# Weight preparation spread over later stages in a one-core attention and MLP kernel

## The chip, the cores and the metric

The kernel runs on one core of a Trainium2 chip. The metric is the device time of one execution in microseconds (us); lower is better. A core has a matrix engine (TensorE, PE in the profile, its weight loads PEld), a vector engine (VectorE, DVE), a scalar engine (ScalarE, ACT), GpSimd (POOL) and SyncE (SP), which here issues almost all transfers. Each engine works through its own queue of instructions in order and waits for the others by semaphores.

## The reference

Eight batches with twelve heads of 448 x 64: queries and keys are normed by their root mean square, attention runs on them, and the result (3584 rows of 768) goes through an MLP with `h - tanh(h)` between its two layers.

```python
q_n, k_n = (rmsnorm(q, g_q), rmsnorm(k, g_k))
scores = scale * np.matmul(q_n, k_n.transpose(0, 1, 3, 2))
attn = np.exp(scores - max); attn = attn / (np.sum(attn) + 1e-09)
attn_out = np.matmul(attn, v)
x = attn_out.transpose(0, 2, 1, 3).reshape(B * S, H * D)
...
h = x @ w_in            # 768 x 2048
g = h - np.tanh(h)
out = (g @ w_out)       # 2048 x 768
```

The two weights come as float64, read as pairs of 32-bit words.

## The kernel before, in words

**Attention in slots.** A slot is one pair of heads of one batch; there are 48 (`steps`). The first six (batch 0) run in `first_slot`, the next six (batch 1) in `early_slot`, the rest in `slot`. A slot holds scores, exponentials, totals (L700, their reciprocal `rs` on VectorE L705), the products with v, and for later slots the loads of q, k and v, the norm (`rr`, L143 to L145, with a power on GpSimd) and the transposes on TensorE (L467, L471). The recording order in the code is the order on each engine; nothing reorders it.

**The MLP as a stream.** `mlp()` is a generator that yields after each matmul. `run(gap)` inside a slot takes so many nanoseconds of it. For the eight batches the stream is hidden(0), project_first(0), hidden(1), project(1), and then pairs of batches. The layers, except project_first, are made from seven products per block (a Strassen-like scheme; `ORDER` is 1, 5, 6, 2, 3, 7, 4), so each needs sums and differences of weight blocks, the combinations. hidden(0) has four sets of seven products; each product is 6 matmuls, 12 instructions on TensorE, and it goes to one of three PSUM banks called mm. Slots 6, 7 and 8 carry hidden(0); slots 9, 10 and 11 carry project_first.

**Preparing the weights.** There are 32 pieces (`PIECES`): 0 to 15 of w_in, 16 to 31 of w_out. Each is loaded raw (768 KB, L290 or L294), passes ScalarE twice (L71, L72), VectorE three times (`round_weight_b`, L78, L79, L82) and GpSimd twice (L92). `weight(to)` starts pieces up to `to`: it puts ScalarE's part of piece n, then by `settle(n)` the VectorE and GpSimd parts of the piece before it, then the loads of pieces ahead. Raw data lies in the later gT buffer for the first `EARLY` pieces, after that in three rotating buffers `w_raw`; a buffer is free again when GpSimd is done with its piece. When four w_in pieces are settled, four combinations are queued (`combine`, L357). The finished w_in blocks are kept in DRAM (`keep_step`, L372), for all later batches.

`EARLY` is 8: `first_slot` asks for pieces up to s + 2, that is 7 by the end of slot 5. In hidden(0) the list `due` says up to which piece the weights are asked for at each of the 28 products: 8 at the first, 16 at the 14th, 24 at the last.

**project_first.** Six chunks of 128 output columns, each summed over 16 row blocks f: 96 matmuls (L1339, two instructions each). Before, chunk follows chunk, the right three first, each in one mm bank: right half from pieces 16 to 23, left half from 24 to 31. Pieces 24 to 31 are asked for over the first 48 matmuls; then `combine_w_out` (L381 to L384) makes four combinations of w_out rows for each of eight f, one f every four matmuls, in two slots of the ring, and they are kept in DRAM (L388). After each chunk ScalarE copies the bank, VectorE transposes it (L966) and SP stores it (four issues, L971).

**The ring.** `ring` has six slots (`SLOTS`). From hidden(1) on every product reads its weights from a ring tile that is loaded from DRAM some products ahead (`ring_load`, issued by SP). Before, project_first loads the first four tiles at matmuls 84 and 86, and each product of hidden(1) then asks for five tiles more than its own number.

**Totals.** In `visit`, used from slot 11 on, slots 11 and 12 take an mm bank for their totals.

Of the kernel before, what the change touches and what calls it, by code (L numbers as in the profile page):

```python
# [147 lines left out]
def bounded_path(tc, ctx, q, k, v, moe_w_in, moe_w_out, out, g_col, ident, ones, half_ones, neg_half, early):  # L148
# [17 lines left out]
    nc = tc.nc  # L166
    B, H, S, D = q.shape
# [47 lines left out]
    def mm_bank():  # L215
        return bank_of("mm")
# [170 lines left out]
    def keep_factors(n, count, f, src):  # L387
        nc.sync.dma_start(  # L388
            out=w_out_dram[:, n : n + count, :, f, :].rearrange("p k c d -> p (k c) d"),
            in_=src[:, : count * HALF].rearrange("p (k d) -> p k d", d=P),  # L390
        )
# [25 lines left out]
            ring_steps += [(first, 2, p, part) for p in outer for part in (1, 2, 3, 4, 0)]  # L417
    ring_tiles = {}

    def ring_load(to):  # L420

        for n in range(len(ring_tiles), min(to, len(ring_steps))):
            b, layer, j, p = ring_steps[n]
            t = ring_tiles[ring_steps[n]] = ring_slot()
            if layer == 0:
                assert kept[1] > j
                nc.sync.dma_start(out=t[:, : 2 * HALF], in_=w_in_dram[j, p])
            elif layer == 2 and p == 0:
                nc.sync.dma_start(out=t, in_=w_out_dram[:, BLOCKS[j], HC - 1].rearrange("p f d -> p (f d)"))
            elif layer == 2:  # L430
                n = min(2 * HB, 7 * HB - 2 * (p - 1) * HB)
                at = 2 * (p - 1) * HB
                nc.sync.dma_start(out=t[:, :n], in_=inner_dram[j][:, at : at + n])
            else:
                nc.sync.dma_start(out=t, in_=w_out_dram[:, BLOCKS[p], j].rearrange("p f d -> p (f d)"))


    normed, turned, probs, sums, whole, xT, tt = {}, {}, {}, {}, {}, {}, {}
# [208 lines left out]
    def visit(s, av):  # L647
# [169 lines left out]
    assert len(due) == 7 * SETS and due[-1] == CF + HF  # L817

    def part(name):
        if name == "th" and "blocks" in late:  # L820
# [60 lines left out]
    def hidden(b):  # L881
# [25 lines left out]
        def done_with(j):  # L907
# [11 lines left out]
            def use(p, bank):  # L919
# [2 lines left out]
                    beside_hidden(b, j, p)  # L922
                if p == 1:
                    nc.scalar.copy(out=s1, in_=v)
                elif p == 5:
                    nc.vector.tensor_tensor(out=s5, in0=v, in1=s1, op=ALU.add)
# [382 lines left out]
    def project_first(b):  # L1309
# [4 lines left out]
        late["todo"] = []  # L1314
        keep_step(0, SETS - 1)
        took = 4 * S / ENGINE_NS
        for m in range(CD * CF):
            k, f = m // CF, m % CF
            n = (k + HC) % CD
            if f == 0:  # L1320
                bank = mm_bank()
            if f == CF // 2:
                step_out(2)
            if k < HC:
                weight(CF + HF + HF * (m + 1) // (HC * CF))
            elif m < HC * CF + 2:
                keep_w_out(PIECES - 2 + m - HC * CF)
            elif (m - HC * CF) % 4 == 0 and m - HC * CF <= 4 * HF:
# [79 lines left out]
    def first_slot(s):  # L1408
# [471 lines left out]
```

## Time and profile before

| what | value |
|---|---|
| median of 3 runs | 1344.65 us (1343.43 to 1344.74) |
| profiled execution, time | 1342.53 us |
| its span on the core | 1340.7 us |
| PE busy | 1311.5 us, 98% |
| DVE busy | 969.5 us, 72% |
| ACT busy | 568.1 us, 42% |
| POOL busy | 795.0 us, 59% |
| TensorE clock granted, mean | 0.998 |
| first six slots on PE | until about 76 us |
| hidden(0) on PE | 76.7 to 172.9 us |
| project_first on PE | 176.3 to 268.6 us |
| hidden(1) starts on PE | 274.5 us |

A busy share is a mean over stages with different limits, so it tells little by itself. A row of a timeline reads: start, length, engine, line, operation, output<-input, shape, count, and in brackets how long the engine had been idle before and what ended that. A row of waits reads: engine, line, tile, what it waited for, then the sum in us, how often, and the longest. A row of windows gives for each engine the busy time and the number of instructions in the stretch, then the granted TensorE clock (1.00 is full speed), the share of the DMA engines that was busy, and GB/s.

### The profile page before, as it was taken

The numbers are of one execution on the slowest core, as the hardware profiler recorded it, in microseconds if no ns is written. First come the engines' busy times: TensorE is split into PE (matmuls) and PEld (weight loads), VectorE is DVE, ScalarE is ACT, GpSimd is POOL, SyncE is SP. The second block draws the span as 40 slices with busy tenths as digits, with TensorE's granted clock in tenths as the row PEclk, the third lists the DMA queues.
The fourth block names the chain that finished last, engine by engine and source line by source line (L and its number), as shares of the span: only waits on it lengthen the run. The fifth ranks groups of instructions, "written<-read, shape, count | busy, mean of one in ns | idle before, by whom it ended". The sixth has DMA issues, their size and how long they took to land.

```text
span 1340.7 us, 29301 instructions
## 1 busy us (share of the span) xinstructions
PE 1311.5 (98%) x11368; PEld 1033.4 (77%) x11368; DVE 969.5 (72%) x1410; ACT 568.1 (42%) x1328; POOL 795.0 (59%) x591
## 2 busy tenths in 40 slices
PE   7989999999999999999999999999999999999997
PEld 3467854488998888688878788779887888799986
DVE  4999978867765767688888576768888667634455
ACT  7856654244343454445322445454512254311102
POOL 4766776348846256726698245944699244812771
PEclk9999999999999999999999999999999999999999
DMA  7779889889999766476655867466745776466544
GB/s 169 183 214 262 265 260 231 250 278 279 340 284 287 181 160 180 112 186 155 171 149 136 201 162 183 117 170 165 181 132 145 150 201 161 118 161 172 170 142 102
DMA packets 364759, 253.53 MB, mean 189 GB/s; under 512 B 273028, under 2 KB 303300, under 8 KB 364612
## 3 DMA queue, kind: packets, MB, share of 16 engines
q1 hardware_dynamic: 364608, 251.57, 69.1%
q8 instruction: 92, 1.51, 0.5%
q14 instruction: 55, 0.45, 0.1%
q10 hardware_dynamic: 4, 0.00, 0.0%
HBM read 205.23 MB, written 46.27 MB: 188 GB/s over the span
## 4 chain that ended last, share of the span: by engine, by line
PE 83%; DVE 7%; POOL 4%; DMA 2%; SPq 2%; issue 2%; ACT 1%; DVEq 0%; ACTq 0%; POOLq 0%
PE mm L857 38%; PE mm L1142 21%; PE sc L569 9%; PE sc L635 6%; PE mm L1339 5%; POOL u L1099 3%; PE sc L623 1%; POOL rr_mine L523 1%; PE sc L677 1%; DVE w_out L357 1%; PE mm L677 1%; SPq L497 1%; DVE rs L705 1%; DMA w_f<-w_inner 1%; DVE w_out L82 0%
## 5 line engine op out<-in xcount | busy, mean ns | idle before, releaser
L857 PE MATMUL mm<-xT,w_f 128*128 128x224 f32 x1296 | 263.5, 353 | 0.8 <-DVE xT L767 0.8
L857 PEld LDWEIGHTS mm<-xT,w_f 128*128 128x128 f32 x1296 | 244.8, 190 | 5.5 <-issue 4.2
L569 PE MATMUL sc<-qT,kT 64*32 64x448 f32 (+1 forms) x3072 | 215.6, 499 | 2.7 <-ACT p_last L575 2.1
L857 PE MATMUL mm<-tt,w_f 128*128 128x224 f32 x1044 | 212.6, 355 | 0.2 <-DMA w_f<-w_in 0.2
L857 PEld LDWEIGHTS mm<-tt,w_f 128*128 128x128 f32 x1044 | 195.8, 190 | 15.9 <-issue 15.4
L523 POOL TENSOR_TENSOR rr_mine<-rr_mine,neg_half 128x28 f32<-128x28 f32 x33 | 162.2, 4915 | 2.7
L762 DVE TENSOR_TENSOR xT<-xT,sc 128x448 f32<-128x448 f32 x34 | 21.0, 618 | 165.8 <-PE sc L569 114.8
L1142 PE MATMUL mm<-u,w_f 128*128 128x224 f32 x672 | 137.2, 354 | 1.0 <-POOL u L1099 0.5
L905 POOL TENSOR_TENSOR gT<-s,th 128x448 f32<-128x448 f32 x44 | 57.8, 1313 | 132.2 <-ACT th L904 128.7
L1142 PE MATMUL mm<-gT,w_f 128*128 128x224 f32 (+3 forms) x512 | 132.0, 412 | 1.2 <-DVE acc L1149 0.9
L1142 PEld LDWEIGHTS mm<-u,w_f 128*128 128x128 f32 x672 | 126.1, 190 | 8.0 <-POOL u L1099 3.6
L569 PEld LDWEIGHTS sc<-qT,kT 64*32 64x32 f32 x3072 | 72.4, 106 | 68.1 <-issue 49.2
L1142 PEld LDWEIGHTS mm<-gT,w_f 128*128 128x128 f32 x512 | 93.9, 190 | 34.3 <-issue 32.0
L635 PE MATMUL sc<-p,v_nat 64*32 64x448 f32 x1184 | 116.9, 536 | 0.0
L1142 PE MATMUL mm<-g,w_f 128*128 128x224 f32 (+1 forms) x360 | 98.9, 428 | 0.0
L575 ACT ACTIVATE p<-sc 128x448 f32<-128x448 f32 x132 | 71.9, 545 | 50.3 <-PE sc L569 37.4
L905 POOL TENSOR_TENSOR g<-s,th 128x448 f32<-128x448 f32 x24 | 30.3, 1264 | 105.1 <-ACT th L904 105.1
L1142 PEld LDWEIGHTS mm<-g,w_f 128*128 128x128 f32 x360 | 67.9, 190 | 26.5 <-issue 26.0
L729 ACT COPY sum_g<-sum 32x14 f32<-32x14 f32 x280 | 56.3, 201 | 72.0 <-DVE sum L721 66.3
L1339 PE MATMUL mm<-gT,w_out 128*128 128x448 f32 x192 | 74.0, 542 | 0.0
L145 POOL TENSOR_TENSOR rr<-rr,neg_half 112x8 f32<-112x8 f32 (+1 forms) x30 | 49.8, 1689 | 35.5 <-DVE rr L144 35.0
L1099 POOL TENSOR_TENSOR u<-gT 128x448 f32<-128x448 f32 x48 | 63.5, 1342 | 11.1 <-PE mm L1142 11.1
(206 smaller groups left out, 2465.8 us busy)
## 6 DMA issues: line engine op xcount, KB each, us to landing
w_f<-w_in SPq DMA_DIRECT2D x196, 384.0 KB, 3.5
w_f<-w_inner SPq DMA_DIRECT2D x63, 512.0 KB, 3.7
w_f<-w_out SPq DMA_DIRECT2D x42, 512.0 KB, 3.9
w_raw<-in_moe_w_out_dram SPq DMA_DIRECT2D x16, 768.0 KB, 5.4
w_in<-w_out SPq DMA_DIRECT2D x21, 384.0 KB, 5.3
qk_nat<-in_q_dram SPq DMA_DIRECT2D x132, 56.0 KB, 2.6
qk_nat<-in_k_dram SPq DMA_DIRECT2D x132, 56.0 KB, 2.4
g<-w_out SPq DMA_DIRECT2D x14, 512.0 KB, 5.4
```

The costliest lines, as they stand in the source:

```text
L145: nc.gpsimd.tensor_tensor(out=r, in0=r, in1=neg_half[:rows], op=ALU.pow)
L523: nc.gpsimd.tensor_tensor(out=mine, in0=mine, in1=neg_half[:, :1].to_broadcast([P, 2 * NJ]), op=ALU.pow)
L569: nc.tensor.matmul(tiles[h][i * BL : (i + 1) * BL, :n], lhsT=kT[r, c * P + at : c * P + at + BL], rhs=qT[r, first : first + n], start=True ...
L575: nc.scalar.activation(p[:, h, c if c < 2 else 0, :], tiles[h][:, :n], AF.Exp, scale=1.0 if rr is None else rr[:, 0, 2 * c + h : 2 * c + h ...
L635: nc.tensor.matmul(av[g][i * BL : (i + 1) * BL, :S], lhsT=v_nat[keys, h, c, m * BL : (m + 1) * BL], rhs=p[keys, h], start=first, stop=True ...
L677: nc.tensor.matmul(av[n][r : r + BL, :HS], lhsT=v_nat[:, h, c, m * BL : (m + 1) * BL], rhs=p[c][:, h, n * HS : (n + 1) * HS], start=False, ...
L729: nc.scalar.copy(out=acc[h * BL : (h + 1) * BL, g], in_=part[g * BL : (g + 1) * BL, h * NJ : (h + 1) * NJ])
L857: nc.tensor.matmul(bank[:, f * HS : (f + 1) * HS], lhsT=w[:, c * width + f, :], rhs=moving[p](c), start=(first and f == 0 and c == 0), sto ...
L905: eng.tensor_tensor(out=g[:, rows, cols], in0=h, in1=th, op=ALU.subtract)
L1099: nc.gpsimd.tensor_tensor(out=u[:, half], in0=a[:, half], in1=z[:, half], op=ALU.subtract)
L1142: nc.tensor.matmul(bank[:, :n], lhsT=w(i), rhs=mv, start=(first and i == 0), stop=(i == len(moving) - 1), skip_group_check=not first,)
L1339: nc.tensor.matmul(bank[:, :S], lhsT=w_out_row(f, n // HC)[:, n % HC * P : (n % HC + 1) * P], rhs=g[:, f, :], start=(f == 0), stop=(f == C ...
```

## The change

- `EARLY` is 5. `first_slot` starts pieces 0 to 4 in slots -1 to 3 and none in slots 4 and 5; `settle` is called in the slot itself.
- `due` in hidden(0) is a list by a new rule: 5 5 6 7 8 8 8, 9 9 10 10 11 12 12, 13 13 14 14 15 16 16, 17 17 18 18 19 19 19. So 14 pieces beside the first layer.
- The last 13 pieces are asked for in project_first by the list `behind`, over its first 58 matmuls.
- project_first works on three chunks at once: for each row block f one matmul into each of the three mm banks, first for the right half, then for the left. The combinations of w_out rows start six matmuls later (58 to 86). The last two of them are written to DRAM in four pieces each instead of two. The three results of a half are copied and stored together.
- The totals of slots 11 and 12 take an sc bank.
- Ring tiles: two are loaded at matmul 92, six by matmul 94, and three more are issued by ScalarE in the first set of hidden(1).

```diff
-    EARLY, PIECES = 8, 2 * CF
+    EARLY, PIECES = 5, 2 * CF
...
-        late["keep"].append(lambda: [keep_factors(3 + 2 * i, 2, f, t[i]) for i in range(2)])
+        if f < HF - 2:
+            late["keep"].append(lambda: [keep_factors(3 + 2 * i, 2, f, t[i]) for i in range(2)])
+            return
+        late["keep"].append(lambda: [keep_factors(3 + n, 1, f, s) for n, s in enumerate((s3, s1, s2, s4))])
...
-    def ring_load(to):
+    def ring_load(to, queue=nc.sync):
...
-            totals(s, mm_bank())
+            totals(s, sc_bank())
...
-    due = [EARLY + (CF - EARLY) * (m + 1) // (7 * SETS // 2) for m in range(7 * SETS // 2)]
-    due += [CF + HF * (m + 1) // (7 * SETS // 2) for m in range(7 * SETS // 2)]
+    SOON_OUT, LAST_OUT = 3, 58
+    due = [min(EARLY + max(m - 1, 0), 8 + max(m - 5, 0) * 4 // 7, CF + SOON_OUT) for m in range(7 * SETS)]
+    behind = [min(PIECES, CF + SOON_OUT + (PIECES - CF - SOON_OUT) * (m + 1) // LAST_OUT) for m in range(CD * CF)]
...
                 if p == 1:
                     nc.scalar.copy(out=s1, in_=v)
+                    if single and j == 0:
+                        ring_load(SLOTS + 1, nc.scalar)
...
                     nc.vector.tensor_tensor(out=s2, in0=v, in1=s1, op=ALU.add)
+                    if single and j == 0:
+                        ring_load(SLOTS + 2, nc.scalar)
                 elif p == 2:
                     shrink(up, low, v, nc.vector)
+                    if single and j == 0:
+                        ring_load(SLOTS + 3, nc.scalar)
...
         for m in range(CD * CF):
-            k, f = m // CF, m % CF
-            n = (k + HC) % CD
-            if f == 0:
-                bank = mm_bank()
-            if f == CF // 2:
-                step_out(2)
-            if k < HC:
-                weight(CF + HF + HF * (m + 1) // (HC * CF))
...
-                combine_w_out((m - HC * CF) // 4 - 1)
-            elif m == CD * CF - 12:
-                ring_load(2)
...
-            elif m == CD * CF - 10:
-                ring_load(4)
+            k, f, i = m // (HC * CF), m % (HC * CF) // HC, m % HC
+            n = (1 - k) * HC + i
+            if m % 4 == 3:
+                step_out()
+            weight(behind[m])
+            if f == 0:
+                bank = [] if i == 0 else bank
+                bank.append(mm_bank())
...
+            if m >= LAST_OUT - 4:
+                keep_combined((m - LAST_OUT + 4) // 4)
...
+            if m == CD * CF - 4:
+                ring_load(2)
+            elif m == CD * CF - 2:
+                ring_load(SLOTS)
             nc.tensor.matmul(
-                bank[:, :S], lhsT=w_out_row(f, n // HC)[:, n % HC * P : (n % HC + 1) * P], rhs=g[:, f, :],
+                bank[i][:, :S], lhsT=w_out_row(f, n // HC)[:, n % HC * P : (n % HC + 1) * P], rhs=g[:, f, :],
                 start=(f == 0), stop=(f == CF - 1),
             )
             if f == CF - 1:
-                y = part("s2").rearrange("p f s -> p (f s)")
-                nc.scalar.copy(out=y, in_=bank[:, :S])
-                store(b, n, y)
+                y = part(("s2", "s5", "s1")[i]).rearrange("p f s -> p (f s)")
+                nc.scalar.copy(out=y, in_=bank[i][:, :S])
+                store(b, n, y, part("s2").rearrange("p f s -> p (f s)") if i == 2 else None)
...
-            weight(s + 2)
+            weight(min(s + 2, EARLY))
+            settle(min(max(s + 1, 0), EARLY))
```

More of the change, by code (lines that the diff above doesn't have):

```diff
@@ L426, in ring_load @@
                 assert kept[1] > j
-                nc.sync.dma_start(out=t[:, : 2 * HALF], in_=w_in_dram[j, p])
+                queue.dma_start(out=t[:, : 2 * HALF], in_=w_in_dram[j, p])
             elif layer == 2 and p == 0:
-                nc.sync.dma_start(out=t, in_=w_out_dram[:, BLOCKS[j], HC - 1].rearrange("p f d -> p (f d)"))
+                queue.dma_start(out=t, in_=w_out_dram[:, BLOCKS[j], HC - 1].rearrange("p f d -> p (f d)"))
             elif layer == 2:
@@ L432, in ring_load @@
                 at = 2 * (p - 1) * HB
-                nc.sync.dma_start(out=t[:, :n], in_=inner_dram[j][:, at : at + n])
+                queue.dma_start(out=t[:, :n], in_=inner_dram[j][:, at : at + n])
             else:
-                nc.sync.dma_start(out=t, in_=w_out_dram[:, BLOCKS[p], j].rearrange("p f d -> p (f d)"))
+                queue.dma_start(out=t, in_=w_out_dram[:, BLOCKS[p], j].rearrange("p f d -> p (f d)"))
     normed, turned, probs, sums, whole, xT, tt = {}, {}, {}, {}, {}, {}, {}
@@ L812, in bounded_path @@
     late = {}
[L815 to L817 removed]
+    SOON_OUT, LAST_OUT = 3, 58
+    due = [min(EARLY + max(m - 1, 0), 8 + max(m - 5, 0) * 4 // 7, CF + SOON_OUT) for m in range(7 * SETS)]
+    behind = [min(PIECES, CF + SOON_OUT + (PIECES - CF - SOON_OUT) * (m + 1) // LAST_OUT) for m in range(CD * CF)]
+    assert due[-1] == CF + SOON_OUT and due[7 * (SETS - 1) - 2] == CF
     def part(name):
@@ L1316, in project_first, with keep_combined @@
         took = 4 * S / ENGINE_NS
-        for m in range(CD * CF):
-            k, f = m // CF, m % CF
-            n = (k + HC) % CD
-            if f == 0:
-                bank = mm_bank()
-            if f == CF // 2:
-                step_out(2)
-            if k < HC:
-                weight(CF + HF + HF * (m + 1) // (HC * CF))
-            elif m < HC * CF + 2:
-                keep_w_out(PIECES - 2 + m - HC * CF)
-            elif (m - HC * CF) % 4 == 0 and m - HC * CF <= 4 * HF:
+        combined = [0]
+        def keep_combined(to):
+            for f in range(combined[0], min(to, HF)):
                 for fn in late["keep"]:
@@ L1331, in project_first @@
                 late["keep"] = []
-                combine_w_out((m - HC * CF) // 4 - 1)
-            elif m == CD * CF - 12:
-                ring_load(2)
+                combine_w_out(f)
+                combined[0] = f + 1
+        for m in range(CD * CF):
+            k, f, i = m // (HC * CF), m % (HC * CF) // HC, m % HC
[6 more added lines that the diff above has]
+                bank.append(mm_bank())
+            if LAST_OUT <= m < LAST_OUT + 2:
+                keep_w_out(PIECES - 2 + m - LAST_OUT)
+            if m >= LAST_OUT - 4:
+                keep_combined((m - LAST_OUT + 4) // 4)
+            if m == CD * CF - 6:
                 for fn in late["keep"]:
                     fn()
-            elif m == CD * CF - 10:
-                ring_load(4)
+                late["keep"] = []
+            if m == CD * CF - 4:
+                ring_load(2)
+            elif m == CD * CF - 2:
+                ring_load(SLOTS)
             nc.tensor.matmul(
-                bank[:, :S], lhsT=w_out_row(f, n // HC)[:, n % HC * P : (n % HC + 1) * P], rhs=g[:, f, :],
+                bank[i][:, :S], lhsT=w_out_row(f, n // HC)[:, n % HC * P : (n % HC + 1) * P], rhs=g[:, f, :],
                 start=(f == 0), stop=(f == CF - 1),
```

## The prediction

> **What bounds the kernel now.** I read the windows first, then who TensorE waited for, then the timelines of the engines around the places found. All times are microseconds of the profiled execution, counted from the start of its span.
>
> ```profile
> core 0: us, PE busy (x) PEld busy (x) DVE busy (x) ACT busy (x) POOL busy (x), PEclk, DMA share, GB/s
> 60.00:70.00 10.00, 8.48 (x164) 4.15 (x167) 9.71 (x15) 7.78 (x14) 9.24 (x8) 1.00 0.82 194
> 80.00:90.00 10.00, 7.04 (x40) 6.34 (x38) 9.76 (x12) 5.72 (x9) 4.66 (x5) 1.00 1.00 284
> 90.00:100.00 10.00, 8.85 (x111) 5.66 (x112) 9.86 (x13) 1.86 (x5) 6.32 (x5) 0.83 0.42 151
> 110.00:120.00 10.00, 8.38 (x88) 6.26 (x80) 9.83 (x13) 4.43 (x12) 9.11 (x7) 1.00 0.98 276
> 140.00:150.00 10.00, 10.00 (x100) 7.83 (x99) 9.79 (x15) 4.20 (x12) 8.06 (x6) 1.00 0.92 290
> ...
> 92.00:94.00 2.00, 2.00 (x14) 1.35 (x20) 1.97 (x2) 0.00 (x0) 0.71 (x1) 0.50 0.40 156
> 94.00:96.00 2.00, 2.00 (x48) 0.98 (x51) 2.00 (x4) 0.79 (x2) 1.75 (x2) 0.71 0.00 0
> ```
>
> From 60 to 124 VectorE (DVE) is full and TensorE (PE) is not; from 130 on PE is full in every window. PE's waits say the same:
>
> ```profile
> PE sc L467 <- DVE rs L705: 3.9, 2, 2.3
> PE mm L857 <- DVE s L926: 2.5, 1, 2.5
> ```
>
> ```profile
> PE mm L1142 <- DVE acc L1149: 0.9, 1, 0.9
> PE mm L857 <- DVE xT L767: 0.8, 1, 0.8
> ```
>
> The second answer covers 130 to the end: all PE waits there sum to 3.0. So PE is the bound of the whole rest, and a shorter stretch ahead of 124 moves the end one for one, unless a new wait appears. PE's timeline has the gaps, DVE's what fills them:
>
> ```profile
> 83.77 0.66 PE L467 MATMUL sc<-ident,qk_nat 128*128 128x128 f32 x4 [1.57 <-DVE rs L705]
> 91.15 2.81 PE L857 MATMUL mm<-xT,w_out 128*128 128x224 f32 x8 [2.54 <-DVE s L926]
> 120.70 0.66 PE L467 MATMUL sc<-ident,qk_nat 128*128 128x128 f32 x4 [2.32 <-DVE rs L705]
> ```
>
> ```profile
> 79.98 0.55 DVE L78 TENSOR_SCALAR w_out<-w_out 128x768 f32<-128x768 f32 x1
> ...
> 82.15 1.56 DVE L705 RECIPROCAL rs<-sc 128x224 f32<-128x224 f32 x1
> ...
> 89.61 0.94 DVE L357 TENSOR_TENSOR w_out<-w_out,w_out 128x768 f32<-128x768 f32 x1
> 90.48 0.61 DVE L926 TENSOR_TENSOR s<-mm,s 128x448 f32<-128x448 f32 x1
> ```
>
> The reciprocal and the sum that PE waits for stand in DVE's queue behind weight pieces (L78, L79, L82: one piece) and their combinations (L357).
>
> **Fewer pieces early: the gain.** Up to the reciprocal at 74.96 the changed program gives DVE the same work (piece 4 is settled in the same slot), so the small gaps before it stay: 1.10 at 65.29, 0.42 at 66.92, 0.47 at 76.66. Then:
> - Piece 5 (79.98 to 82.15, 2.17) leaves the place before the reciprocal. That starts at 79.98, ends about 81.5; PE is free at 82.2. The gap of 1.57 goes.
> - Pieces 6 and 7 (83.63 to 89.61) and a combination (0.94) leave the place before the sum at 90.48. Its product ends on PE about 81.2, so the sum is done about 82.1. The gap of 2.54 goes.
> - The granted clock fell right after that gap: 0.50 in 92 to 94, 0.71 in 94 to 96, 0.97 in 88 to 92. Lost: 2 x 0.50 + 2 x 0.29 + 4 x 0.03 = 1.7. Without the gap I take it as gone.
> - By the reciprocal at 119.09 the old order has settled 8 pieces since 76.5 and made 7 combinations; the new due list (8 at products 5 and 6, 9 at 7 and 8) makes 4 of each. At 2.2 to 2.9 a piece and 0.94 to 1.3 a combination DVE has about 4 x 2.5 + 3 x 1.1 = 13 less to do, PE's clock is 5.8 earlier, so the reciprocal comes about 5 in time. The gap of 2.32 goes.
> Sum: 1.57 + 2.54 + 1.7 + 2.32 = 8.1. Bounds: 0 (another DVE operation holds the same places) to 8.1 + 2.0 (the small gaps go as well).
>
> [...]
>
> **What comes just in time.** A set of four pieces is now settled one to two products ahead of its first use. At product 12 to 14 DVE has a piece (2.5) and a combination (1.1) after the results of product 12: 3.6, and the combination is read by product 15, three products of 12 x 0.19 = 2.3 later. Hidden: cost 0, bound 1.5 (one late combination for each of the three sets, 0.5 each). Cover gone: 1.1 a combination.
>
> **Thirteen pieces in the second layer: the cost.** Five more pieces between 176 and 236. VectorE: L78, L79 and L82 have means of 0.755, 0.830, 1.218 there, so 2.8 a piece, 14.0; DVE is busy 13.99 + 18.58 + 17.49 of the 60 from 180 to 240, so 9.9 lie free, and one combination of w_out rows (four operations, 2.2 to 3.1) moves behind: 1 to 2 overflow. ScalarE 5 x 1.8 and GpSimd 5 x 2.0 to 2.6 fit in their free 27 and 22. What is tight is the raw buffer, of which there are three: load, ScalarE, VectorE, GpSimd, next load.
>
> ```profile
> 188.29 0.37 SPq L294 DMA_DIRECT2D w_raw<-in_moe_w_out_dram  x1
> ...
> 194.76 0.94 ACT L71 ACTIVATE w_out<-w_raw 128x768 f32<-128x768 f32 x1
> ...
> 203.22 2.62 POOL L92 TENSOR_TENSOR w_out<-w_out,w_raw 128x384 int32<-128x384 int32 x2 [2.14 <-issue]
> ...
> 205.87 0.37 SPq L294 DMA_DIRECT2D w_raw<-in_moe_w_out_dram  x1
> ```
>
> This round took 17.6; the one from 201.11 to 216.09 took 15.0; bare it is 5.2 + 1.8 + 2.1 + 2.0 = 11.1. The new list asks 13 pieces over 58 matmuls (about 179 to 232 on the old axis): 13 per round of three. The three raw buffers are full at the start; loads 22 to 31 run in rounds from about 188. With 15.0, load 31 goes out at 188.3 + 45 = 233.3, reaches ScalarE 5.4 later, is scaled at 240.5, settled on VectorE at 243.3. Behind it in DVE's queue stand the first combination (2.2), the sums of squares (1.7), GpSimd's power (3.3) and the scaled rows (0.65): 251.1. PE transposes those at 250.14. Late by 1.0; with 11.1 not late (0), with 17.6 late by 8.8. Nearest is 15.0, since the old list itself asked only one piece in 5.6, which stretched these rounds. I take 1.5 with the overflow, bounds 0 and 8.8.
>
> **Three banks at once.** PE's work stays 192 instructions. A bank's copy (0.53 on ScalarE) must end before its next use: between the halves an attention part of 4.2 lies between (221.02 to 225.26), after the end the next slot's 5.9 (268.58 to 274.53). Cost 0; cover gone, 0.5 to 1.6 each time. All three results are stored in one go: 12 issues of 0.6 on SP, behind them the next q and k loads, some 8 later than at 277; their squares stand on ScalarE with sums read from SBUF behind them, so PE feels nothing until its bank needs the copy of the next set, 6 later.
>
> [...]
>
> **Ring loads.** SP issues six together at the end of the layer, behind eight stores of w_out sums (four more issues than before, 0.6 each). The last combination ends near 262.6 on the old axis (xT at 247.2, five combinations of 2.2, rows 2.2, one more); issues until 266, landing 5.6 later: 272. PE needs the first at 274.5. Cost 0, bounds 0 and 2. Three more are issued from ScalarE (0.2 to 0.5 each, as its two at the start: 0.51, 0.21) into a stretch where it is busy 7.9 of 20: 0. The reciprocal's sums of two slots move to an sc bank, free once the exponentials of chunk 1 are read (242.6, PE there at 242.98): 0, bounds 0 and 0.8. A raw load one slot earlier: 768 KB at about 230 GB/s is 3.3 in slots of 8.66 whose DMA share is 0.76; the q and k rows have a whole slot in hand: 0.
>
> **Sum.** -8.1 + 1.5 = -6.6. The profiled execution, 1342.53 (span 1340.7 and 1.8 around it), would become 1335.9. It lies 2.1 under the median of the runs; applied to 1344.65 this gives 1338.0.
>
> **Rivals.**
> - More is freed: the three small gaps go too and nothing is late: -10.1, 1334.5. For: less work on ScalarE in the slots. Against: DVE's queue before 74.96 is unchanged. 0.13.
> - DVE stays late in the first layer: the last gap (2.32) and half of the clock loss stay, 1.5 more for combinations in time: about -3.6, 1341. For: DVE is still some 92% full (9.3 products, 5 pieces, 4 combinations and attention are 28.5 of a slot of 31). 0.13.
> - The gain is given back in the second layer: rounds near 17.4 eat 8: 1344.6. For: two of the three rounds measured took 17.6. Against: they were stretched by the list. 0.13.
> - Slower: the three raw buffers set the pace. Price 1.0 + 3 x (round - 15.0), against 8.1; from a round of 17.4 it decides, at 19 it costs 13.0: +4.9, 1349.5. For: ScalarE already waited 25.8 for raw loads in seven waits between 76 and 280. Against: DMA share there is 0.83 to 0.92 with room. 0.11.
> - The forecast, 1338.0, own range 1336 to 1341: 0.50.
>
> **How the numbers follow.** 0.2% is 2.7 us, about what a measurement can tell from no change. Faster: 0.50 + 0.13 + 0.13 = 0.76; within: 0.13; slower: 0.11. The range takes in 1334.5 less 1.0 and the given-back case: 1333.5 to 1345, leaving the slower case and a little of the rest out.
>
> **What would show it.** Right: windows from 77 to 124 with PE full and the clock at 1.00, no wait on rs L705 or s L926 longer than 0.5 there, hidden(1) starting 6 to 8 earlier. Wrong: PE waits on rows or scaled rows between 215 and 250, ScalarE's waits for w_raw far above 25.8 in sum, PE waiting for w_f at the start of the second block, or the granted clock below 1 in the second layer.

## The result, and the profile after

| | before | changed |
|---|---|---|
| median of runs | 1344.6 us (6 runs, 1341.57 to 1344.74) | 1358.55 us (6 runs, 1353.06 to 1360.84) |
| ratio, 95% interval | 1 | 1.0108 (1.0094 to 1.0122) |
| span of the profiled execution | 1340.7 us | 1358.0 us |
| granted TensorE clock, mean | 0.998 | 0.99 |

The changed kernel is 1.1% slower, where 0.5% less (1338.0) was forecast. Three executions of the kernel before, beside the run e18_seq2 below, took 3539 to 4554 us; they are left out of every median and ratio here. Windows of the changed kernel first (same columns as before the prediction):

```profile
core 0: us, PE busy (x) PEld busy (x) DVE busy (x) ACT busy (x) POOL busy (x), PEclk, DMA share, GB/s
80.00:100.00 20.00, 20.00 (x184) 17.56 (x183) 16.24 (x27) 11.23 (x19) 6.32 (x6) 1.00 0.50 132
100.00:120.00 20.00, 20.00 (x163) 17.51 (x169) 18.15 (x24) 12.81 (x26) 14.17 (x11) 1.00 0.87 232
120.00:140.00 20.00, 20.00 (x225) 15.41 (x214) 19.31 (x27) 10.68 (x17) 14.29 (x12) 1.00 1.00 290
150.00:152.00 2.00, 1.98 (x5) 1.84 (x6) 2.00 (x3) 2.00 (x5) 2.00 (x2) 0.50 0.97 376
152.00:154.00 2.00, 2.00 (x7) 1.78 (x7) 1.97 (x2) 1.66 (x3) 2.00 (x3) 0.50 0.69 181
154.00:156.00 2.00, 2.00 (x7) 1.60 (x5) 1.97 (x2) 0.00 (x0) 1.35 (x1) 0.50 0.80 183
156.00:158.00 2.00, 2.00 (x53) 1.14 (x56) 2.00 (x4) 0.78 (x2) 1.71 (x2) 0.98 0.97 351
...
227.00:229.00 2.00, 1.45 (x14) 0.18 (x14) 2.00 (x4) 0.83 (x3) 0.00 (x0) 0.69 0.94 227
229.00:231.00 2.00, 2.00 (x10) 1.08 (x4) 1.89 (x5) 1.80 (x3) 0.06 (x1) 0.50 1.09 367
```

From 80 to 140 PE is full at full clock: the three gaps of before are gone, as predicted. At 150 the clock is at half for six microseconds, and it falls again at 227. PE's waits from 130 to the end, which summed to 3.0 before, say what is new:

```profile
PE mm L861 <- DVE s L943: 7.0, 1, 7.0
PE sc L572 <- ACT p_last L578: 3.0, 1, 3.0
PE mm L861 <- DVE w_out L357: 3.0, 1, 3.0
PE mm L861 <- DMA w_f<-w_in: 2.6, 2, 2.0
```

PE's timeline gives their places:

```profile
150.02 6.27 PE L861 MATMUL mm<-tt,w_out 128*128 128x224 f32 x16 [2.97 <-DVE w_out L357]
...
227.55 1.62 PE L572 MATMUL sc<-qT,kT 64*32 64x448 f32 x14 [3.04 <-ACT p_last L578]
...
307.68 6.70 PE L861 MATMUL mm<-tt,w_f 128*128 128x224 f32 x20 [7.00 <-DVE s L943]
```

Sixteen such matmuls take 3.19 at full clock, twenty 3.95: the gaps at 150 and 308 were each followed by about 3 us of lost clock (6.27 - 3.19, 6.70 - 3.95). Behind the gap at 227 the windows show 0.69 and 0.50 for two microseconds each: 2 x 0.31 + 2 x 0.50, about 1.6 lost.

To add this up I take PE's transposes of q and k (L470, before L467) as milestones, numbered from 0 (the very first, which read the tile `rows`, is not counted); no. 7 lies early in slot 6, where hidden(0) runs, no. 10 lies at the start of project_first, no. 13 at the start of hidden(1). The expectations below call them the transposes of slot n, with this number. Changed minus before, in us: no. 6 +1.6, no. 9 -7.6, no. 10 -1.7, no. 11 -1.7, no. 12 +5.4, no. 13 +7.0, end of the span +17.3. So 9.2 is won between no. 6 and no. 9, then 5.9 lost around 150, 7.0 between no. 11 and 12 (second layer), 1.7 behind it, and 10.3 from the start of hidden(1) on. The two profiled executions differ by 17.3, the medians by 14.0: of each kernel one execution was profiled, that of the kernel before lies 2.1 under the median of its six runs, that of the changed kernel 1.2 over its own.

**The wait at 227.** ScalarE's timeline in the changed kernel:

```profile
204.40 0.97 ACT L71 ACTIVATE w_out<-w_raw 128x768 f32<-128x768 f32 x1 [7.98 <-DMA w_raw<-in_moe_w_out_dram]
...
224.19 0.90 ACT L71 ACTIVATE w_out<-w_raw 128x768 f32<-128x768 f32 x1 [3.30 <-DMA w_raw<-in_moe_w_out_dram]
224.99 0.88 ACT L72 ACTIVATE w_raw<-w_raw 128x768 int32<-128x768 uint32 x1
225.76 1.39 ACT L1364 COPY s<-mm 128x448 f32<-128x448 f32 x3
227.02 0.81 ACT L578 ACTIVATE p_last<-sc,rr 128x224 f32<-128x224 f32 x2
```

The exponentials that PE waits for (p_last) stand behind a weight piece (L71, L72) whose raw data isn't there yet, and behind the copies of three banks. PE does not wait for the piece or for the copies at that moment (its next matmuls into these banks come behind the scores, at 229.1); it waits since p_last stands behind them in ScalarE's queue. Of the 7.0 between no. 11 and 12, this wait is 3.0, a wait for p at 213.7 is 0.7, and the fall of the clock about 1.6; the rest is not split further.

**The wait at 308.** SP and VectorE in the changed kernel:

```profile
276.37 5.00 SPq L430 DMA_DIRECT2D w_f<-w_in  x6
281.42 1.76 SPq L117 DMA_DIRECT2D v_nat<-in_v_dram  x2
283.23 1.74 SPq L127 DMA_DIRECT2D v_nat<-in_v_dram  x2
285.56 6.11 SPq L981 DMA_DIRECT2D out_dram<-th  x8
291.78 1.00 SPq L1038 DMA_DIRECT2D g<-w_out  x2
293.43 2.91 SPq L981 DMA_DIRECT2D out_dram<-s  x4
296.38 3.72 SPq L500 DMA_DIRECT2D qk_nat<-in_q_dram  x4
300.15 2.04 SPq L500 DMA_DIRECT2D qk_nat<-in_k_dram  x4
```

```profile
305.48 1.08 DVE L511 TENSOR_REDUCE rr_mine<-sum_T 128x28 f32<-128x896 f32 x1 [10.95 <-ACT sum_T L504]
306.48 0.61 DVE L942 TENSOR_TENSOR s<-mm,s 128x448 f32<-128x448 f32 x1
307.01 0.61 DVE L943 TENSOR_TENSOR s<-mm,s 128x448 f32<-128x448 f32 x1
```

SP comes to the q and k loads at 296.4, 19.4 later than in the kernel before (277.0), behind six ring loads and the twelve stores of three chunks. The sums of their squares reach VectorE at 305.5; there the next step (L511) stands ahead of the two sums (L942, L943) that PE's next product needs. VectorE stands idle for 10.95 in front of it, and PE for 7.0.

Where do the 19.4 come from? Before its ring loads SP stores the combinations of w_out rows. The last of these stores and the end of the last combination on VectorE, in the changed kernel:

```profile
270.13 6.19 SPq L391 DMA_DIRECT2D w_out<-w_f  x8
274.74 0.56 DVE L384 TENSOR_TENSOR w_f<-w_out,w_f 128x384 f32<-128x384 f32 x1
```

In the kernel before, the first ring loads, the end of the last combination and the q loads:

```profile
258.30 1.48 SPq L427 DMA_DIRECT2D w_f<-w_in  x2
259.51 0.56 DVE L384 TENSOR_TENSOR w_f<-w_out,w_f 128x384 f32<-128x384 f32 x1
277.01 4.10 SPq L497 DMA_DIRECT2D qk_nat<-in_q_dram  x4
```

The last combination ends at 275.3 instead of 260.1, so 15.2 of the 19.4 are there before SP comes to its first ring load. PE itself is 6.3 late by then (its scores start at 274.9 instead of 268.5); the other 8.9 is VectorE's. From there to the q loads it is 21.1 instead of 16.9: the longer pile of ring loads and stores adds 4.1.

### The profile page after: what moved, and what is told of

Read it like the earlier page. It is cut to its first block, busy times and chain, and to the rows that moved or that the text cites. A ratio compares the mean times of both kernels' runs of the same rounds, so it can differ in the third digit from the quotient of the medians.

```text
span 1358.0 us, 29291 instructions
## 1 busy us (share of the span) xinstructions
PE 1319.1 (97%) x11368; PEld 1038.1 (76%) x11368; DVE 968.6 (71%) x1410; ACT 567.8 (42%) x1328; POOL 789.2 (58%) x591
## 4 chain that ended last, share of the span: by engine, by line
PE 78%; DVE 9%; POOL 5%; DMA 4%; issue 2%; SPq 2%; ACT 1%; DVEq 0%; ACTq 0%; POOLq 0%
PE mm L861 38%; PE mm L1152 20%; PE sc L572 8%; PE sc L638 6%; POOL u L1109 2%; PE mm L1358 2%; PE sc L626 1%; POOL rr_mine L526 1%; DMA w_f<-w_in 1%; PE mm L680 1%; DVE w_out L357 1%; DVE rows L616 1%; DVE w_out L82 1%; PE mm L703 1%; PE sc L680 1%
## 5 line engine op out<-in xcount | busy, mean ns | idle before, releaser
L861 PE MATMUL mm<-tt,w_f 128*128 128x224 f32 x1044 | 215.5, 358 | 7.0 <-DVE s L943 7.0
L861 PEld LDWEIGHTS mm<-tt,w_f 128*128 128x128 f32 x1044 | 197.8, 192 | 23.5 <-issue 15.4
L92 POOL TENSOR_TENSOR w_out<-w_out,w_raw 128x384 int32<-128x384 int32 x46 | 57.3, 1266 | 49.2 <-ACT th L908 15.4
```

The costliest lines, as they stand in the source:

```text
L92: nc.gpsimd.tensor_tensor(out=bits[:, part], in0=bits[:, part], in1=raw[:, part, 0], op=ALU.add)
L861: nc.tensor.matmul(bank[:, f * HS : (f + 1) * HS], lhsT=w[:, c * width + f, :], rhs=moving[p](c), start=(first and f == 0 and c == 0), sto ...
```

## The experiments

All positions are PE milestones minus those of the kernel before, from one profiled execution of each kernel; the medians are of all its runs, the ratio is to the kernel before on the same chip. The start of the span scatters by up to 0.8 (no. 4), and a profiled execution can lie off the median of its kernel: that of e5_sp lies 5.1 over it, that of e10_even5 2.9 under it.

| run | no. 6 | no. 9 | no. 10 | no. 11 | no. 12 | no. 13 | end | median us | ratio (95%) |
|---|---|---|---|---|---|---|---|---|---|
| changed | 1.6 | -7.6 | -1.7 | -1.7 | 5.4 | 7.0 | 17.3 | 1358.55 | 1.0108 (1.0094 to 1.0122) |
| e1_front | 2.8 | 8.9 | 8.6 | 8.6 | 8.6 | 8.6 | 7.6 | 1351.18 | 1.0073 (1.0048 to 1.0097) |
| e2_back | 0.0 | -0.1 | -0.4 | -0.4 | 6.6 | 8.3 | 17.9 | 1360.51 | 1.0125 (1.0108 to 1.0142) |
| e3_lead | 1.6 | -1.3 | -0.2 | -0.2 | 7.9 | 8.3 | 18.7 | 1360.95 | 1.0129 (1.0107 to 1.0151) |
| e5_sp | 3.1 | -5.0 | -0.5 | -0.5 | 6.9 | 7.9 | 21.6 | 1359.02 | 1.0117 (1.0100 to 1.0134) |
| e6_qk | 3.2 | -6.1 | -3.2 | -3.2 | 4.5 | 5.7 | 13.9 | 1355.88 | 1.0098 (1.0077 to 1.0119) |
| e7_sums | 1.9 | -6.6 | -3.7 | -3.7 | 4.4 | 4.4 | 16.0 | 1356.93 | 1.0095 (1.0078 to 1.0112) |
| e8_three | 0.7 | 1.6 | 1.3 | 1.3 | 1.3 | 1.3 | 7.1 | 1349.96 | 1.0052 (1.0035 to 1.0069) |
| e9_all | 2.4 | -5.7 | -4.1 | -4.0 | 3.4 | 3.8 | 11.5 | 1354.04 | 1.0075 (1.0052 to 1.0098) |
| e10_even5 | 3.0 | -4.2 | 2.5 | 3.3 | 3.3 | 3.3 | 1.8 | 1347.23 | 1.0028 (1.0013 to 1.0042) |
| e11_even6 | 1.0 | -4.2 | 2.6 | 3.3 | 3.3 | 3.3 | 4.9 | 1345.99 | 1.0017 (1.0007 to 1.0027) |
| e12_act | 3.0 | -5.6 | -2.7 | -2.7 | 11.5 | 11.6 | 21.6 | 1364.78 | 1.0165 (1.0141 to 1.0189) |
| e13_ten | 2.7 | -5.4 | 1.7 | 1.7 | 1.8 | 1.8 | 10.3 | 1354.05 | 1.0085 (1.0063 to 1.0108) |
| e15_load | 0.2 | -9.0 | -6.2 | -6.2 | 1.4 | 2.3 | 12.0 | 1355.72 | 1.0101 (1.0077 to 1.0125) |
| e14_pairs | -0.1 | -9.3 | -7.7 | -5.4 | -1.0 | -0.8 | 0.7 | 1344.66 | 1.0013 (1.0003 to 1.0023) |
| e16_pairs20 | 0.2 | -9.0 | -7.4 | -5.4 | 8.8 | 9.0 | 11.3 | 1354.36 | 1.0073 (1.0049 to 1.0096) |
| e17_seq | 0.0 | -9.2 | -7.6 | -7.6 | -7.6 | -1.3 | 5.2 | 1346.93 | 1.0022 (1.0010 to 1.0034) |
| e18_seq2 | 0.0 | -9.2 | -7.6 | -7.6 | -7.1 | -6.5 | -2.9 | 1340.07 | 0.9980 (0.9971 to 0.9989) |
| e19_ring | 1.0 | -8.2 | -6.6 | -6.5 | -6.2 | -5.4 | -0.3 | 1342.16 | 0.9997 (0.9988 to 1.0006) |

### The change cut in two, and two small edits

**e1_front**, the front alone on the kernel before:

```diff
-    EARLY, PIECES = 8, 2 * CF
+    EARLY, PIECES = 5, 2 * CF
-            weight(s + 2)
+            weight(min(s + 2, EARLY))
+            settle(min(max(s + 1, 0), EARLY))
```

> The kernel before with the front part alone: five pieces in the first six slots, then a ramp that still reaches 16 at product 14 and 24 at the last product; second layer as before. Theory A (the early slots cost 9 us and nothing of the front part costs anything): the three TensorE gaps between 80 and 124 go, hidden(1) starts 6 to 9 earlier than 274.5, the time is 1336 to 1339. Rival B (VectorE is simply full, so work taken out early comes back as waits between 124 and 175): the gaps go but others of 4 to 9 us in sum appear before 175, 1341 to 1346.

Both missed: slower than before. The old list still asks for 16 pieces by the 14th product, so eleven pieces come in fourteen products. ScalarE's timeline of this run at the longest gap (6.31 on PE at 137):

```profile
134.84 0.91 ACT L71 ACTIVATE w_out<-w_raw 128x768 f32<-128x768 f32 x1 [4.84 <-DMA w_raw<-in_moe_w_in_dram]
135.65 0.89 ACT L72 ACTIVATE w_raw<-w_raw 128x768 int32<-128x768 uint32 x1
136.44 0.56 ACT L904 ACTIVATE th<-s 128x448 f32<-128x448 f32 x1
136.91 0.76 ACT L575 ACTIVATE p_last<-sc,rr 128x224 f32<-128x224 f32 x2
```

It is the pattern of 227: a piece without its raw data, and p_last behind it. To watch VectorE alone was not enough.

**e2_back**, the changed kernel with the old front:

```diff
-    EARLY, PIECES = 5, 2 * CF
+    EARLY, PIECES = 8, 2 * CF
-    due = [min(EARLY + max(m - 1, 0), 8 + max(m - 5, 0) * 4 // 7, CF + SOON_OUT) for m in range(7 * SETS)]
+    due = [EARLY + (CF - EARLY) * (m + 1) // (7 * SETS // 2) for m in range(7 * SETS // 2)]
+    due += [CF + SOON_OUT * (m + 1) // (7 * SETS // 2) for m in range(7 * SETS // 2)]
```

> The changed kernel with the old front (eight pieces early, 16 at product 14, then only 19 by the end of the first layer): the second-layer part alone. Theory A (the loss is made in the second layer and at the start of the second block, whatever the front does): 8 lost between the start of project_first and hidden(1), about 10 in the first set of hidden(1), no wait for a combination near 150, time 1360 to 1364. Rival B (the loss is made because the shortened front hands late pieces on): second layer without new waits, 1344 to 1348.

Theory A. The loss of the second layer and of hidden(1) is there in full without the new front: 7.0 between no. 11 and 12, 9.6 from no. 13 on.

**e3_lead**, sets of pieces asked two products sooner (`8 + max(m - 3, 0) * 4 // 7` in `due`), and **e5_sp**, the three ring loads of ScalarE back on SP (`ring_load(SLOTS + 1)` to `+ 3` without `nc.scalar`):

> The changed kernel with each set of four pieces asked for two products sooner (slope starts at product 3 instead of 5). Theory A (the wait of 3.0 for a combination near 150 and the clock dip of 3.1 behind it come from too short a lead): both go, hidden(0) ends 6 earlier, 1351 to 1354. Rival B (VectorE has no room, so a sooner request only moves the wait): sum of TensorE waits before 175 stays at 3 or above, 1357 to 1361.

> The changed kernel with the three extra ring loads issued by SP instead of ScalarE. Theory A (the 7.0 wait at 307 comes from q and k loads that stand behind stores in SP's queue, themselves late because the combinations of w_out rows end late): the wait stays at 6 or more, 1357 to 1362. Rival B (the loads issued by ScalarE tie SP's stores to ScalarE, and that makes the q and k loads late): the wait falls below 3 and the clock dip goes, 1348 to 1352.

Neither gains: Rival B in e3_lead, and in e5_sp the time of Theory A without its wait. In e3_lead the wait at 150 is gone, but at no. 9 it has 6.3 less in hand than the changed kernel: five waits of 0.5 to 1.2 between 105 and 140 took its place. In e5_sp the wait on s (7.0) is gone too and PE waits 8.6 for ring tiles instead.

### The three waits, one by one

**e6_qk**, the q and k loads of step 15 sooner:

```diff
-                (following, lambda: add_third(s + 1)), (first, lambda: load_blocks(s + 3)),
+                (following, lambda: add_third(s + 1)),
...
+        if s == HALVED:
+            load_blocks(s + 4)
```

> The changed kernel with one edit: the q and k loads of step 15 are issued at the end of slot 11, ahead of the third-chunk stores and inside slot 12 no more. Theory A (in the first set of hidden(1) VectorE stands 10.95 behind the squares of rows that SP issued last, behind ring loads and twelve stores): the wait of 7.0 on s and the clock dip of 2.75 after it go, 1358.6 - 9.8 = about 1349 (1347 to 1351). Rival B (everything SP issues there is late alike, and the ring loads or the squares' neighbours then end last): the wait moves, 1354 to 1360.

Rival B: the wait on s went, others took its place, and from no. 13 to the end 8.2 are lost in place of 10.3. ScalarE's timeline in this run shows the next wait:

```profile
283.57 0.53 ACT L928 COPY s<-mm 128x448 f32<-128x448 f32 x1
...
295.25 0.54 ACT L908 ACTIVATE th<-mm 128x448 f32<-128x448 f32 x1 [11.15 <-DMA out_dram<-th]
```

The tanh writes the tile that still holds a result of the second layer, and its store is now what SP issues last; PE waits 6.8 in eight places for ring tiles as well.

**e7_sums**, GpSimd's sums of x rows (L812) at the end of each slot:

```diff
-            x_sums(b, (c,), range(4), nc.vector if b == 0 and c == HC - 1 else nc.gpsimd)
+            fn = lambda: x_sums(b, (c,), range(4), nc.vector if b == 0 and c == HC - 1 else nc.gpsimd)
+            late.setdefault("sums", []).append(fn) if b else fn()
...
+        for fn in late.pop("sums", []):
+            fn()
```

> The changed kernel with one edit: GpSimd's sums of x rows for the second batch are recorded at the end of each slot instead of right behind the division. Theory A (the two raw rounds of 25 and 21 are long since GpSimd's last part of a piece stands behind these sums): ScalarE's waits for raw data of 8.0 and 7.4 shrink to about 5, the waits on p_last and p in the second layer (3.0 and 0.7) and the dip after them go, 1352 to 1355. Rival B (DMA, SP or the list sets the pace): 1357 to 1361.

Theory A falls; the time (1356.93) is just under Rival B's range. In the changed kernel the sums did hold GpSimd's part of a piece up (to 195.7, after a wait of 3.3 for xT), but without that the second layer still loses 8.1 (no. 11 to 12), p_last waits 4.3.

**e9_all**, both edits and pieces 14 to 16 one product sooner (`due[15:20] = 14, 14, 15, 16, 16`):

> The changed kernel with three edits: the q and k loads as in the run e6_qk, the sums as in e7_sums, and pieces 14 to 16 of the first layer asked for one product sooner. Theory A (the three waits are independent, each with its clock dip: 9.8 in hidden(1), 5 in the second layer, 6 at 150): 1358.6 - 9.8 - 5 - 5 = 1338 to 1343, at or below the kernel before. Rival B (one wait gives way to the next): 1347 to 1358.

Rival B, by time. The wait at 150 went and no. 10 stands 2.4 sooner than in the changed kernel, but p_last waits 4.5 in the second layer and 7.7 are lost after no. 13.

**e12_act**, e6_qk with the 24 stores of the second layer issued by ScalarE (`queue = nc.sync if b else nc.scalar` in `store`):

> The changed kernel with the q and k loads as in e6_qk, and the stores of the second layer's results (24 issues) from ScalarE instead of SP. Theory A (SP's queue at the end of the second layer is what hurts hidden(1): 18 stores of combinations, six ring loads, twelve stores of results in front of everything): with the stores out of it the wait of tanh on the stored tile (11.1 in e6_qk) and most of the 6.8 on ring loads go, 1347 to 1351. Rival B (the transfers themselves or the late combinations set the end): 1354 to 1358.

Both missed, the slowest of all. ScalarE's queue stood still with the stores, by the trace for earlier stores of the same tiles, and behind them stands what PE waits for (here kT; s L928 after it had PE wait 7.8):

```profile
292.21 7.98 ACTq L982 DMA_DIRECT2D out_dram<-th  x8
300.23 0.63 ACT L472 ACTIVATE kT<-sc,g_col 128x448 f32<-128x448 f32 x1 [12.93 <-DMA out_dram<-th]
```

### How many pieces, and how many chunks

**e8_three**: the changed kernel with `EARLY` 8, the old `due`, and `SOON_OUT, LAST_OUT = 8, 58`: three chunks at once, eight pieces in the second layer. **e13_ten**: the changed front up to 16, then `due[20:] = 16, 17, 18, 19, 20, 20, 21, 22`, ten pieces in the second layer.

> The changed kernel with the weight lists of before: eight pieces early, 24 by the end of the first layer, eight in the second; three chunks at once, stores and ring loads as changed. Theory A (the five more pieces are what costs in the second layer, and they are what makes the ring loads and the q and k loads late): second layer as before, wait on s in hidden(1) of 2 or less, 1342 to 1347. Rival B (the three chunks at once cost by themselves: twelve stores and six ring loads ahead of the q and k loads): the second layer as before, but 7.0 + 2.8 lost in hidden(1), 1352 to 1356.

> The changed kernel with three pieces moved back: 17 beside the first layer (16, 17, 18, 19, 20, 20, 21, 22 over its last eight products) and ten in the second, in the same 58 matmuls. Theory A (13 pieces in 58 matmuls outrun three raw buffers, ScalarE then stands in front of p_last): ten do not, the 7.0 between the transposes of slots 11 and 12 fall to 2 or less, VectorE is done with the combinations earlier and hidden(1) loses some 4 less: 1347 to 1352 if the first layer holds. Rival B (the order of work in the second layer costs, not the count): 1355 to 1360.

From no. 11 to 12 the kernel before takes 35.47, eight pieces 35.46, ten 35.49, thirteen 42.51 and (e2_back) 42.46. So eight or ten pieces in 58 matmuls cost nothing in this stretch and thirteen cost 7, with the old front (e2_back) as with the new one. Behind no. 13 eight pieces with three chunks lose 5.8, ten lose 8.5, thirteen 10.3 (one profile each): more than half of it is there without the five extra pieces, the rest grows with them. That half need not be the pile on SP alone: in e8_three too, where the pieces are asked over ten matmuls more and the combinations six matmuls later, the last combination ends late, at 268.4 (8.3 later than before, PE 1.3 of it); SP comes to the q loads at 288.5. No run moves the combinations alone, so their share and that of the pile are not told apart. By time both runs lie between their theories; e13_ten came out above Theory A since its first layer lost 7.1 between no. 9 and 10.

**e10_even5** and **e11_even6**: the kernel before with five or six early pieces and `due` evenly spread up to 24; the second layer untouched.

> The kernel before with five pieces in the first six slots and a list of due pieces that rises evenly over the first layer (8 at product 4, 12 at 11, 16 at 18, 24 at 28); second layer, ring and stores as before. Theory A (the first layer has the room, the changed kernel only gave its gain away later): the gaps of before at 83.8, 91.2 and 120.7 go, nothing new over 1, 1336 to 1340. Rival B (VectorE has no room for 19 pieces beside the first layer, whatever the spacing): new gaps there worth as much as the old ones, 1343 to 1350.

> As e10_even5, but six pieces in the first six slots, 18 beside the first layer. Theory A: the gap at 91.2 goes, that at 120.7 shrinks, 1337 to 1341. Rival B (VectorE without room): 1342 to 1348, nearer to the kernel before than e10_even5.

Rival B for both. 7.2 and 5.2 are won between no. 6 and 9, and 6.7 and 6.8 lost again by no. 10: at 162 p_last has PE wait 3.1 in e10_even5, behind a piece for whose raw data ScalarE had waited 2.27.

**e15_load**, the changed kernel with the raw loads of pieces 5 to 7 a slot later:

```diff
-            load_weights(n + (3 if n < EARLY - 3 else 4))
+            load_weights(n + (3 if n < EARLY else 4))
...
+            if s + 1 >= EARLY - 1:
+                load_weights(s + 4)
```

> The changed kernel with one edit: the raw loads of pieces 5 to 7 go out a slot later, as in the kernel before. Theory A (these loads stand ahead of the q rows on SP and on the transfers; ScalarE waited some 3 for q rows in the six-slot stage): slots 4 to 6 take 18.5 again instead of 19.4 to 21.5, the whole is 1 to 3 shorter, 1355 to 1357. Rival B (the q rows are late for another reason, or a later wait takes it back): within 1 of the changed kernel, 1358 to 1360.

Theory A in the place it speaks of: from no. 4 to 6 it takes 18.71 (before 18.49); in ten profiles with five early pieces and the loads sooner it took 19.4 to 21.9, in e10_even5 with ScalarE waiting 3.03 for q rows at 52.6. Of the five runs below with the later loads, four took 18.5 to 18.7, but e19_ring 19.3, with a wait of 1.1 for q rows: the order of the loads is not all of it. The whole time fits the expectation, but its interval overlaps that of the changed kernel.

### Towards a version that keeps the gain

**e14_pairs** and **e16_pairs20**: the kernel before with five early pieces, the load order of e15_load, and a second layer of two chunks at once, then the third, with ring loads (4) and single stores as before; 11 or 12 pieces in it.

```diff
+        for left in range(2):
+            order += [(left, i, f) for f in range(CF) for i in range(2)] + [(left, 2, f) for f in range(CF)]
+        starts = [2, 8, 14, 20, 25, 30, 35, 40, 45, 50, 54]
+        for m, (left, i, f) in enumerate(order):
...
+            weight(SOON_TO + sum(at <= m for at in starts))
```

> The kernel before with five early pieces, their raw loads as before, the changed kernel's list up to 16 with pieces 14 to 16 a product sooner, 21 by the end of the first layer, and 11 pieces in a second layer that works on two chunks at once, then on the third, with single stores and four ring loads at its end. Theory A (what costs is the pile of stores and ring loads at the end of a layer of three chunks at once, and 13 pieces in 58 matmuls): 6 to 7 gained ahead of the second layer, 0 to 2 lost in it, hidden(1) as before: 1337 to 1342. Rival B (any move of pieces into the second layer makes VectorE late for the combinations, hence the ring): 1345 to 1352.

> As e14_pairs with 20 pieces by the end of the first layer and 12 in the second. Theory A: 1337 to 1343; the waits on p_last in the second layer come back if 12 pieces are too many for three raw buffers (then 2 to 4 more than e14_pairs). Rival B: 1346 to 1354.

e14_pairs lies between the theories: hidden(1) loses 1.5 instead of 5.8 to 10.3, but two places in the second layer give back 6.7. PE there waits 2.61 for GpSimd's part of a piece at 231.7 and is slower behind it: its next eight matmuls took 4.85, the 24 ahead of the wait 9.29. With one piece more (e16_pairs20) such waits are 4.12 and 3.92 in one slot, and from no. 11 to 12 it takes 49.6; its time is above both ranges, by 0.4 in Rival B's case. Its pieces are also asked at other matmuls than those of e14_pairs.

**e17_seq**: left pieces in the order of rows, pieces asked away from the exponentials (`starts = [1, 6, 17, 22, 28, 34, 41, 49, 54, 58, 66]`), VectorE's part three matmuls later, the sums as in e7_sums. **e18_seq2**: `starts = [1, 6, 17, 22, 27, 32, 37, 42, 49, 53, 58]`, combinations two matmuls sooner.

> As e14_pairs, but the left pieces come in order of the rows, so that none is needed before its place in the pair of chunks; the 11 pieces are asked at matmuls 1, 6, 17, 22, 28, 34, 41, 49, 54, 58, 66, away from the p_last exponentials, VectorE's part three matmuls after ScalarE's; the sums of x rows stand at the end of the slots; combinations two matmuls later. Theory A (the second layer lost 6.6 to two places, a late piece with its clock dip and a piece ahead of p_last): both go, hidden(1) starts 4 to 7 sooner than before, 1336.5 to 1341. Rival B (VectorE and the raw buffers are short of time in the second layer, so the waits come back at other places or as a late ring): 1343 to 1350.

> As e17_seq with the last seven pieces asked sooner (27, 32, 37, 42, 49, 53, 58 in place of 28, 34, 41, 49, 54, 58, 66) and the combinations two matmuls sooner. Theory A (the last piece was late: 2.3 at 248 and 3.2 on the first ring tile, each with a clock dip): both go, hidden(1) starts 5 to 7 sooner than before, 1337 to 1341. Rival B (the raw buffers put the piece ahead of a p_last again, or the ring stays late): 1343 to 1348.

Rival B in e17_seq: it keeps all up to no. 12, then its last piece is late: waits of 2.29 at 248 and of 3.20 on the first ring tile. e18_seq2, Theory A, asks for it sooner and is the fastest of all kernels here: 1340.07 against 1342.87, ratio 0.9980 (0.9971 to 0.9989). A PE timeline line of it and its windows of the second layer:

```profile
284.44 2.51 PE L856 MATMUL mm<-tt,w_f 128*128 128x224 f32 x12 [1.76 <-DMA w_f<-w_in]
```

```profile
200.00:240.00 40.00, 40.00 (x330) 19.86 (x315) 33.88 (x43) 23.25 (x42) 22.64 (x21) 1.00 0.91 244
240.00:260.00 20.00, 20.00 (x60) 10.29 (x59) 19.63 (x34) 3.17 (x6) 3.90 (x5) 1.00 0.89 255
```

PE is full through the second layer. Of the 6.5 at no. 13, 2.9 arrive at the end; the rest goes in waits for ring tiles (4.1 in five places).

**e19_ring**, e18_seq2 with ring tiles 7 to 9 loaded by ScalarE, as in the changed kernel:

> As e18_seq2, with ring tiles 7 to 9 loaded from ScalarE in the first set of hidden(1), as in the changed kernel. Theory A (SP's order holds the ring loads up behind the q and k loads, 1.8 at 284 and 1.0 at 314 with the dips behind them): the wait at 284 goes, 1337 to 1339. Rival B (the transfers are full there, 340 GB/s from 280 to 300, and the wait stays or moves to the squares of the q and k rows): 1339.5 to 1342.

Nearest to Rival B, 0.2 above its range: the wait at 284 went, others of 0.9 and 1.8 came at 321 and 342. What bounds the ring there stays open. A fourth raw buffer was not tried.

## Why the prediction was wrong

- **The gain (8.1).** Right in mechanism and place: the three gaps and the dip went, and 9.2 was won from no. 6 to no. 9. One reading was too broad: PE is full from 100 to 110 in the kernel before, and VectorE is busy for only 2.44 of the 4.00 from 120 to 124; the places of the three gaps are right.
- **"A raw load one slot earlier ... the q and k rows have a whole slot in hand: 0".** Wrong by 0.9 in the changed kernel's profile and up to 3.4 in others; in e15_load 0.2 of it is left.
- **"What comes just in time": cost 0, bound 1.5.** Mis-sized. The result was 5.9: one combination of the last set was 2.97 late and the clock dip behind it cost 3.1. The step reckoned VectorE's work alone. In the trace VectorE had been waiting for ScalarE's part of the piece at 145.9, and ScalarE had come to it late (144.9) behind rows and exponentials that had waited for GpSimd.
- **"Thirteen pieces in the second layer": 1.5, bounds 0 and 8.8.** Mis-sized: 7.0, inside its bounds by luck, since the bounds were worked out for another wait. The rounds of the raw buffer for loads 22 to 31 took 12.4 to 19.7, on both sides of the 15.0 that I took, and ScalarE's waits for raw data of w_out pieces sum to 23.5 between 76 and 280 (before: 25.8), so the sign that I named, a sum far above 25.8, did not show. What failed is where a late piece hurts: I followed it to the end of the list (load 31, the transposes at 250), while it hurts at once, in the middle, since p_last stands behind it on ScalarE. A mean round or a sum of waits says nothing about that.
- **"Three banks at once ... PE feels nothing until its bank needs the copy of the next set, 6 later": cost 0, and "Ring loads": cost 0, bounds 0 and 2.** The step that decided, 10.3. Its first term, "The last combination ends near 262.6", measured 275.3. The work behind xT was sized rightly (15.4 reckoned, 15.5 measured); what failed is its start, 247.2, taken from the old profile, when VectorE came to it at 259.8. Of these 12.6, 5.4 is PE's lateness at no. 12, and the rest is VectorE, which the last weight pieces and the first combinations kept full. So SP's queue began its ring loads 18.1 later, and the q and k loads came 19.4 later instead of "some 8". The prediction also put the twelve stores and the six ring loads in two paragraphs and never added them up on SP's queue; that is 4.1 of the 19.4. And it named the squares' place on ScalarE, but not the step behind them on VectorE, which stands ahead of two sums that PE needs. e6_qk shows that the late q and k loads alone are not the whole 10.3: with them early, 8.2 are still lost, in waits for ring tiles and for a tile still being stored. e8_three has 5.8 of it without the five extra pieces.
- **The rivals.** "Slower: the three raw buffers set the pace" had the right resource and a price in the right range for the second layer alone; no rival had late combinations and SP's queue, though the section on what would show an error named the wait for ring tiles.
- **The clock.** The prediction priced the old dip as a gain and no new dip as a cost. Three new ones cost 3.1, about 1.6 and 2.75.

## What to carry to other kernels

Follow an in-order queue past the late instruction: what matters is which instruction of another stage stands behind it and who waits for that, and this holds for the queue that issues transfers as for an engine (in the changed kernel p_last behind a weight piece on ScalarE, 3.04 of PE at 227, and the q and k loads behind stores on SP, 7.00 at 308). When several edits each add a little to one queue, add them on that queue, in issue order, before calling any of them hidden, and start the sum where the engine that feeds the queue will be, not where it was in the old profile. Work that only has to be done sometime should be asked for where its data is already there and where nothing urgent comes next; here eleven pieces in the second layer cost 6.9 from no. 10 to 13 with one list and 1.1 with another (which changed the order of the pieces and the place of GpSimd's sums as well).

## What the hardware showed that was not expected

The same gap does not always cost the same clock. In the changed kernel the gap of 2.97 at 150 was followed by half clock to 156. In e6_qk a gap of 2.90 at the same place was followed by none:

```profile
152.00:154.00 2.00, 2.00 (x12) 2.00 (x11) 2.00 (x2) 2.00 (x4) 2.00 (x3) 1.00 1.02 407
154.00:156.00 2.00, 2.00 (x45) 1.21 (x47) 1.93 (x3) 1.96 (x4) 2.00 (x2) 1.00 0.75 120
```

Its sixteen matmuls took 3.29, and so they did in e7_sums, after 2.96, and in e12_act, after 2.90; in e13_ten, after 2.90, they took 4.73 (clock 0.50 from 152 to 154, 0.72 from 154 to 156), in e5_sp, after 2.96, 4.84. So a gap near 3 us at this place cost itself and between 0.1 and 3.1 more, and no run here shows what decides. Where the changed kernel worked on three PSUM banks in turn without a gap, from 180 to 200 (PE busy 20.00 of 20), the clock was 1.00.
